# Gated linear attention and a three-way maxout FFN on one core: steps of 128 tokens of two batches in place of 256 tokens of one

## The chip, the core and the metric

The kernel runs on one core of a Trainium2 chip. Its engines are TensorE (PE, with PEld for the loading of weights), VectorE (DVE), ScalarE (ACT), GpSimd (POOL) and SyncE (SP), and each takes its instructions in order. The DMA engines are shared and are fed by queues; here SP and ACT issue transfers. The metric is the device time of one execution in microseconds (us).

## What is computed

```python
def _attn_ref(q, k, v, alpha):            # each (4, 8, 768, 48): batch, head, token, dim
    state = np.zeros((B, H, D, D))
    for t in range(S):
        state = alpha[:, :, t, :, None] * state + np.einsum('bhd,bhe->bhde', k[:, :, t], v[:, :, t])
        y[:, :, t] = np.einsum('bhd,bhde->bhe', q[:, :, t], state)
    return y

# x = y, heads side by side: 3072 tokens of 384
h = np.maximum(np.maximum(x @ w1, x @ w2), x @ w3)     # w1, w2, w3: (384, 768)
return h @ w_out                                       # w_out: (768, 384)
```

A linear attention with a decay `alpha` for each token and key dimension, and behind it a feed-forward layer whose hidden value is the largest of three products. Inputs and outputs are float32.

## The kernel before

**Tiling.** A unit is 128 tokens of one batch. Inside it, two neighbouring tokens (R = 2) lie in the free dimension of one partition, so a unit takes 64 partitions, and a tile of 128 partitions holds two units (U = 2). A step `s` is such a tile: 256 tokens in a row of one batch, `c, b = divmod(s, B)`. There are 12 steps: the first 256 tokens of the four batches, then the second, then the third. The two units of a step follow each other in time, so unit 1 needs the state that unit 0 leaves.

**One step.** Each of alpha, k, q and v comes as one load of 384 KB into a ring of four buffers (`load_step`, L94, letter `l`, indices 0 to 3). alpha gives pair products (`m`, L177), logs (`N`, L181) and an inverse (`r`, L186 and L188); a matmul sums the logs (`c`, L202 and L205); `e`, `f` and `g` (L210, L216, L222) take exponentials into the decays for k and q and the gates of the whole unit (`ge`). k and q are scaled (`u`, `w`, `k`, `q`; L192, L196, L228) into float16 tiles, v likewise (`V`, L149), and k and q are turned, by PE and a copy (`T`, `t`) or by a DMA transpose (`D`, L260). Scores (`A`, L273) are masked (`a`, L280). Attention into `yps` has three sources: the state that the other unit's place holds (`X`, `attend_crossed`), the own one and the masked scores (`Y`, `attend`), all on L299; the result is copied to `xT` (`x`).

**The state.** `S` (`update`, L369) multiplies k and v of each unit into `sps`. `s` (`add_state`, L379) adds what was kept, `M` (`gates`, L356) makes the factor `gm`, `z` (`decay_state`, L384) multiplies by it into `kept`, and `y` (`spread_state`, helper lines L143 and L145) copies that as float16 into `st` for the next unit. All four exist once per unit, with tiles of 128x192 for the state; the second unit of the last chunk is left out, which makes 20 of each.

**The feed-forward layer.** `G` (`gate`, L398) is a group of six matmuls of 256 columns for two of the six blocks of 128 hidden units and one of the three weights: index `i` stands for block pair `i // 3` and weight `i % 3`, so each step has nine groups. `h` (`maxed`) casts the first of three to float16 (L143 on ACT, L145 on DVE) and takes the maximum with the others on DVE (L415). `O` (`project`, L424) multiplies with `w_out`, `o` (`store`) scales by a column and sends 128 rows out on SP (L430 by way of L149, L432). Weights come in twelve blocks (`K`, L105 and L108) and are cast to float16 (`W`).

**What sets the order.** The schedule is manual. `ORDER` is a list of pieces, each a letter, an index, an optional engine (`v` DVE, `p` POOL, `a` ACT) and the step: `z0p@3` is the decay of unit 0 of step 3 on POOL. `emit` issues them one after another, so on every engine and in SP's queue the instructions stand in the order of the list. PSUM has eight banks that all results share. `H` pieces are matmuls on zeros.

Of the kernel before, what the change touches and what calls it, by code (L numbers as in the profile page):

```python
# [23 lines left out]
def kernel(  # L24
# [28 lines left out]
    NS = NT // W  # L53
    NQ = 4
    assert DM == H * D and NT == B * S and 2 * D == 3 * C and DM % P == 0
    assert S % W == 0 and U * J == P and (MID + 1) % R == 0
# [35 lines left out]
    def load(n, s):  # L92
        c, b = divmod(s, B)
        nc.sync.dma_start(  # L94
            rings[n][s % NQ].rearrange("j h r d -> j h (r d)"),
            ins[n][b, :, c * W:(c + 1) * W].rearrange("h (j r) d -> j h (r d)", r=R))

    def load_step(s, i, _):
        load("akqv"[i], s)

    def load_weight(i):
        if i < 9:
            w = (moe_w1, moe_w2, moe_w3)[i % 3]
            src = w.rearrange("(f p) j -> p f j", p=P)[:, :, i // 3 * 2 * P:(i // 3 + 1) * 2 * P]
            nc.sync.dma_start(stage[i].rearrange("p (f c) -> p f c", f=NF), src)  # L105
        else:
            src = moe_w_out.rearrange("(j p) m -> p j m", p=P)[:, 2 * (i - 9):2 * (i - 8)]
            nc.sync.dma_start(stage[i].rearrange("p (j m) -> p j m", j=2), src)  # L108
# [18 lines left out]
    sts = [[cpool.tile([P, 2 * HP + 1, D], FP16, name=f"st{b}_{i}") for i in range(2)] for b in range(B)]  # L127

    def clear_padding():
        for st in (st for pair in sts for st in pair):  # L130
            nc.vector.memset(st[:, ::2], 0.0)
        for la in las:
            nc.vector.memset(la.rearrange("p a b c -> p (a b) c")[:, :, D:], 0.0)
        for qk, vt in zip(qks, vts):
            nc.gpsimd.memset(qk.rearrange("p r i a b c -> p (r i a b) c")[:, :, D:], 0.0)
            nc.vector.memset(vt.rearrange("p a b c -> p (a b) c")[:, :, D:], 0.0)
# [83 lines left out]
    def totals(s, *_):  # L220
        gate_of[s] = work.tile([P, HP, U, 2], FP32, name="ge", tag="ge", bufs=8)
# [62 lines left out]
    def held(s, i, x, at, n):  # L284

        b, rows = s % B, slice(64 * i, 64 * (i + 1))
        st = sts[b][x].rearrange("p a d -> p (a d)")
# [16 lines left out]
    def has_state(s, x):  # L304
        return U * (s // B) + x > 0

    def attend_crossed(s, *_):
        for x in range(U):
            y_of[s, x] = bank([P, NF, P], "yps")
        for f in range(NF):  # L310
            for half in range(2):
                at = P * f + 64 * half
                for i in range(2):
                    if has_state(s, 1 - i):
                        for p, st in held(s, i, 1 - i, at, 64):
                            attend_product(s, 1 - i, at, 64, st, asked(s, i, 1 - i, p))

    def attend(s, _, tag):
        vt = vts[s % NQ]
        lats = [lat_of.pop((s, u)) for u in range(U)]  # L320

        def jobs(x, m):
            todo, fs = [], sorted(range(NF), key=lambda f: (P // C * f + m) % 3 == 1)
            fs = [fs[0], fs[2], fs[1]]
            for f in fs if has_state(s, x) else ():
# [27 lines left out]
    def gates(s, x, eng):  # L353
        nxt = gate_of[s][:, :, 1, 0] if x == 0 else gate_of[s + B][:, :, 0, 0]
        gm = work.tile([P, HP], FP32, name="gm", tag="gm", bufs=6)
        engines[eng or "p"].tensor_mul(gm, gate_of[s][:, :, x, 1], nxt)  # L356
        gm_of[s, x] = gm

    def update(s, _, tag):
        qk, vt = qks[s % NQ], vts[s % NQ]  # L360
        xs = range(U) if s + B < NS else range(1)
        for x in xs:
            sps_of[s, x] = bank([P, HP, D], "sps")
        for p in range(HP):
            for r in range(R):
                for x in xs:
# [5 lines left out]
    def add_state(s, x, eng):  # L372
        c, b = divmod(s, B)
        full = work.tile([P, HP, D], FP32, name="full", tag="full", bufs=4)
        full_of[s, x] = full
        if U * c + x == 0:
            copy(eng or "v", full, sps_of.pop((s, x)))
        else:
            nc.vector.tensor_add(full, sps_of.pop((s, x)), kept_of[b, U * c + x - 1])  # L379

    def decay_state(s, x, eng):
        c, b = divmod(s, B)
        kept = kept_of[b, U * c + x] = work.tile([P, HP, D], FP32, name="kept", tag="kept", bufs=6)
        engines[eng or "p"].tensor_mul(kept, full_of.pop((s, x)),  # L384
                                       gm_of.pop((s, x)).unsqueeze(2).broadcast_to([P, HP, D]))

    def spread_state(s, x, eng):
        c, b = divmod(s, B)
        copy(eng or "a", sts[b][1 - x][:, 1::2], kept_of[b, U * c + x])
# [37 lines left out]
    def store(s, x, eng):  # L427
        c, b = divmod(s, B)
        ob = work.tile([P, DM], FP32, name="ob", tag="ob", bufs=5)
        times(eng or "a", ob, ops_of.pop((s, x)), ys_c)  # L430
        row = b * S + (U * c + x) * P
        nc.sync.dma_start(out[row:row + P, :], ob)  # L432

    def warm(_, n, *x):
# [5 lines left out]
        "l": load_step, "K": lambda _, i, *x: load_weight(i), "W": cast_weight, "H": warm,  # L440
# [8 lines left out]
    def emit(order):  # L449
# [6 lines left out]
        l0@0 r0@0 m0v@0 N0@0 H12@0 c0@0 e0@0 l0@1 m0p@1 r0@1 l1@0 u0v@0 k0v@0 r1@0 l2@0 w0v@0  # L456
        N0@1 H8@0 c0@1 f0@0 k1p@0 r1@1 q1v@0 H4@0 T1@0 l0@2 m0v@2 q0v@0 T0@0 f0@1 l2@1 w0v@1
        l1@1 q1v@1 l3@0 N0@2 c0@2 l0@3 l2@2 l1@2 g0@0 r0@2 r1@2 t0v@0 g0@1 l3@1 e0@1 t1v@0 H5@0
        A1@0 K3@0 k1v@1 T1@1 u0p@1 M0p@0 f0@2 a3@0 l3@2 V0a@0 g0@2 q0p@1 t1a@1 k0v@1 A0@0 a0@0
        a1@0 M0p@1 S0@0 s0a@0 T0@1 t0a@1 H4@0 A0@1 m0p@3 z0p@0 s1v@0 a2@0 y0a@0 X0@0 A1@1 N0@3  # L460
        K0@0 q1v@2 c0@3 e0@2 e0@3 a3@1 w0p@2 q0v@2 V0a@1 l2@3 Y0@0 x0a@0 a0@1 x1v@0 W3a@0 f0@3
        u0p@2 k0p@2 g0@3 H5@0 S0@1 s0v@1 T0@2 a1@1 G3@0 k1p@2 a2@1 K1@0 z0p@1 K2@0 y0a@1 h3a@0
        T1@2 s1v@1 V0v@2 X0@1 Y0@1 S0@2 t0a@2 t1v@2 A0@2 A1@2 W0p@0 x1a@1 q1p@3 s0a@2 a1@2 a3@2
        G0@0 a2@2 M0p@2 z0v@2 x0a@1 G3@1 h0v@0 l1@3 M0p@3 G0@1 a0@2 W1a@0 G1@0 l0@5 r0@3 r1@3
        W2p@0 G1@1 y0a@2 X0@2 Y0@2 G2@1 s1v@2 K4@0 w0p@3 q0p@3 G2@0 k1p@3 h1v@0 K6@0 W6p@0 u0v@3
        k0v@3 x1a@2 x0a@2 G2@2 G0@2 h2v@0 W4a@0 G1@2 h0a@1 h1v@1 m0p@5 h2v@1 h0a@2 h1v@2 G4@0
        h4v@0 K7@0 l3@3 V0a@3 T1@3 t1v@3 G6@1 T0@3 t0v@3 G6@2 G4@1 h2v@2 h6a@1 A0@3 h3a@1 h4v@1
        l0@4 m0p@4 W7a@0 G6@0 a0@3 K5@0 W5p@0 G5@0 N0@4 K8@0 a1@3 W8p@0 l1@4 N0@5 c0@5 r0@4
        h6a@0 h5v@0 c0@4 e0@4 A1@3 a3@3 S0@3 s0a@3 G8@2 a2@3 u0p@4 g0@4 z0v@3 k0p@4 G7@0 r1@4
        M1p@0 k1p@4 h7v@0 g0@5 f0@4 K9@0 l2@4 y0a@3 f0@5 s1v@3 h6a@2 M0p@4 w0v@4 G5@1 h5v@1 G8@0  # L470
        h8v@0 l3@4 V0a@4 l1@5 q0p@4 e0@5 X0@3 Y0@3 x1a@3 x0a@3 q1v@4 G7@1 T0@4 t0a@4 l0@6 r0@6
        M1p@1 T1@4 G0@3 S0@4 z1p@0 h7v@1 u0p@5 M0p@5 t1v@4 r0@5 s0v@4 K11@0 A0@4 z0p@4 A1@4 a1@4
        r1@6 l0@7 l0@8 a2@4 a0@4 a3@4 k1p@5 l2@5 K10@0 G3@2 l3@5 G5@2 G1@3 G4@2 y0p@4 m0p@6
        k0p@5 h3a@2 h4v@2 h5v@2 y1a@0 X0@4 Y0@4 h0a@3 r1@5 m0v@7 w0p@5 G7@2 h7v@2 l2@8 l1@6 l2@6
        q1p@5 D1@5 G8@1 h8v@1 h1v@3 x0a@4 x1a@4 G6@3 h6v@3 q0p@5 W11p@0 h8v@2 V0a@5 D0@5 G2@4
        G8@3 G0@4 G1@4 G3@3 N0@6 c0@6 N0@7 h0v@4 h1v@4 W10a@0 W9p@0 s1v@4 z1p@1 f0@6 w0v@6 S0@5
        s0v@5 q0v@6 e0@6 c0@7 f0@7 g0@7 M1p@3 u0v@6 k0p@6 l2@7 l3@6 O0@1 h3a@3 o0a@1 D0@6 l1@7
        q1p@6 k1p@6 O1@2 D1@6 z0v@5 s1v@5 g0@6 M1p@2 o1a@2 e0@7 O0@0 o0a@0 A1@5 a3@5 A0@5 a1@5
        G3@4 G2@3 y1a@1 l1@8 O1@1 r0@8 l0@9 a0@5 l3@8 a2@5 h2v@3 G7@3 G5@4 h7v@3 o1a@1 h8v@3
        y0p@5 O0@2 X0@5 q1p@7 V0a@6 S0@6 Y0@5 m0p@8 z1p@2 r1@8 w0v@8 h2v@4 s0v@6 M0v@6 G4@4  # L480
        h3v@4 h4v@4 G4@3 h4v@3 z0p@6 r0@7 N0@8 r1@7 w0p@7 o0a@2 x1a@5 u0v@7 l0@10 x0a@5 G6@5
        h6a@5 l0@11 r0@9 G7@5 h5v@4 A1@6 a2@6 a3@6 A0@6 a0@6 a1@6 G5@3 s1v@6 y1v@2 G0@5 k0p@7
        G1@5 h0a@5 h1v@5 y0p@6 G3@5 h3a@5 h5v@3 G2@5 M0v@7 X0@6 Y0@6 x1v@6 x0a@6 c0@8 e0@8 G5@5
        f0@8 l3@7 r0@11 q0v@8 u0p@8 k0v@8 G4@5 g0@8 k1p@7 G3@6 l1@9 h4v@5 h3a@6 G4@6 V0a@7 z1v@3
        O1@0 q0p@7 D0@7 M1p@4 z1p@4 G7@6 D1@7 h2v@5 G5@6 l3@10 o1a@0 h5v@5 h4v@6 q1p@8 k1p@8
        S0@7 s0v@7 y1a@4 z0v@7 G0@6 h0a@6 O0@3 D0@8 h7v@5 s1v@7 A0@7 a0@7 D1@8 A1@7 G6@6 V0a@8
        G8@5 m0p@10 l2@9 a2@7 o0a@3 y1p@3 a1@7 h8v@5 h6a@6 G8@6 m0p@9 N0@9 c0@9 f0@9 G6@4 N0@10
        g0@9 M0p@9 M1p@5 y0p@7 O1@3 a3@7 G2@6 h7v@6 X0@7 M0p@8 m0p@11 o1a@3 h6a@4 e0@9 k1p@9
        h5v@6 h8v@6 Y0@7 x1v@7 A1@8 a2@8 x0a@7 r1@9 S0@8 w0p@9 a3@8 r0@10 l2@10 A0@8 G1@6 h1v@6
        a1@8 G0@7 G2@7 G6@7 h2v@6 h6a@7 G7@7 a0@8 G3@7 s0v@8 q0v@9 z0v@8 q1p@9 u0p@9 r1@10 l3@11  # L490
        G5@7 w0p@10 h7v@7 G7@4 G8@7 l1@10 h3a@7 y0a@8 G8@4 l1@11 G4@7 h7v@4 h8v@4 h0a@7 G1@7
        h1v@7 N0@11 l3@9 c0@10 e0@10 X0@8 Y0@8 f0@10 u0p@10 k0p@9 D1@9 q0v@10 x1a@8 l2@11 k0p@10
        x0v@8 V0a@9 O0@5 D0@9 O1@5 o0a@5 c0@11 r1@11 g0@10 z1p@5 G0@8 e0@11 k1p@11 q1p@10 D0@10
# [49 lines left out]
```

## Time and profile before

Three runs took 155.5, 153.03 and 154.42 us, median 154.42.

| of the profiled execution | |
|---|---|
| its own time | 153.8 us |
| span in the profile | 152.0 us |
| mean granted TensorE clock | 0.998 |
| busy: PE / PEld / DVE / ACT / POOL | 140.6 / 107.6 / 117.1 / 86.6 / 76.1 us |
| moved by DMA | 32.52 MB, mean 214 GB/s |
| queue of SP (q1) | 72,576 packets, 84.6% of 16 engines' span |
| 648 matmuls of the expert groups, L398 | 76.2 us busy |
| 144 matmuls of the projection, L424 | 25.7 us busy |

Shares are of the span. The span is measured inside the profiled execution, from the first instruction to the last; the execution's own time is 1.8 us longer. A busy engine is not one at its peak, since matmuls overlap. In lists of groups the columns are line, engine, operation, output and inputs with their shapes and count, then busy time, the mean of one in ns, and the idle time just before with what ended it.

### The profile page before, as it was taken

The numbers are of one execution on the slowest core, as the hardware profiler recorded it, in microseconds if no ns is written. First come the engines' busy times: TensorE is split into PE (matmuls) and PEld (weight loads), VectorE is DVE, ScalarE is ACT, GpSimd is POOL, SyncE is SP. The second block draws the span as 40 slices with busy tenths as digits, with TensorE's granted clock in tenths as the row PEclk, the third lists the DMA queues.
The fourth block names the chain that finished last, engine by engine and source line by source line (L and its number), as shares of the span: only waits on it lengthen the run. The fifth ranks groups of instructions, "written<-read, shape, count | busy, mean of one in ns | idle before, by whom it ended". The sixth has DMA issues, their size and how long they took to land.

```text
span 152.0 us, 6282 instructions
## 1 busy us (share of the span) xinstructions
PE 140.6 (93%) x2722; PEld 107.6 (71%) x2722; DVE 117.1 (77%) x212; ACT 86.6 (57%) x177; POOL 76.1 (50%) x109
## 2 busy tenths in 40 slices
PE   6977969899998999899899999999999999999990
PEld 2434647689786887478688778887878887878650
DVE  5299895899998897699967988969986960977820
ACT  3667968555879377847347666269853406031371
POOL 5327782792698976683736728665865020000000
PEclk9999999999999999999999999999999999999999
DMA  4999999998999999999999999999968301112235
GB/s 121 317 323 306 242 298 334 248 347 236 348 261 308 312 302 207 192 302 257 316 269 240 220 163 293 285 236 196 149 163 44 87 4 56 52 32 76 92 140 182
DMA packets 72891, 32.52 MB, mean 214 GB/s; under 512 B 65440, under 2 KB 72864, under 8 KB 72864
## 3 DMA queue, kind: packets, MB, share of 16 engines
q1 hardware_dynamic: 72576, 31.99, 84.6%
q8 instruction: 21, 0.34, 0.9%
q10 hardware_dynamic: 288, 0.13, 0.5%
q14 instruction: 6, 0.05, 0.1%
HBM read 23.73 MB, written 4.72 MB: 187 GB/s over the span
## 4 chain that ended last, share of the span: by engine, by line
PE 69%; SPq 9%; DMA 7%; POOL 6%; DVE 2%; issue 2%; ACT 2%; DVEq 0%; ACTq 0%; POOLq 0%
PE gps L398 41%; PE ops L424 14%; SPq L94 9%; PE yps L299 6%; DMA ws<-in_moe_w_dram 4%; PE aps L273 3%; POOL qk L228 3%; DMA qkT<-qk 3%; PE sps L369 2%; PE tps L252 2%; DVE h L415 1%; POOL wo L145 1%; PE lps L202 1%; POOL ka L192 1%; POOL qa L196 1%
## 5 line engine op out<-in xcount | busy, mean ns | idle before, releaser
L398 PE MATMUL gps<-xT,wcat 128*128 128x256 f16 x648 | 76.2, 273 | 1.7 <-ACT wcat L143 0.8
L398 PEld LDWEIGHTS <-wcat 128*128 128x128 f16 x648 | 61.5, 98 | 11.2 <-ACT wcat L143 1.3
L280 DVE TENSOR_TENSOR lat<-aps,cp 128x512 f16<-128x512 f32 x48 | 30.6, 683 | 3.8 <-PE aps L273 3.5
L415 DVE TENSOR_TENSOR hT<-gps,h 128x512 f16<-128x512 f32 x36 | 24.0, 686 | 9.7 <-PE gps L398 5.4
L415 DVE TENSOR_TENSOR h<-gps,h 128x512 f16<-128x512 f32 x36 | 24.4, 687 | 4.1 <-PE gps L398 1.8
L143 ACT CAST h<-gps 128x512 f16<-128x512 f32 x28 | 16.3, 587 | 18.2 <-PE gps L398 12.2
L424 PE MATMUL ops<-wo,hT 128*128 128x384 f16 x144 | 25.7, 326 | 0.3 <-ACT h L143 0.3
L149 ACT ACTIVATE ob<-ops,c 128x384 f32<-128x384 f32 x24 | 13.8, 582 | 17.0 <-PE ops L424 17.0
L424 PEld LDWEIGHTS <-hT 128*128 128x128 f16 x144 | 13.8, 98 | 8.4 <-issue 0.5
L143 ACT CAST xT<-yps 128x384 f16<-128x384 f32 x20 | 8.9, 480 | 9.8 <-PE yps L299 9.6
L384 POOL TENSOR_TENSOR kept<-full,gm 128x192 f32<-128x192 f32 x14 | 8.0, 570 | 10.9 <-PE aps L273 4.9
L149 ACT ACTIVATE vt<-rv,c 128x768 f16<-128x768 f32 x11 | 10.3, 936 | 4.3 <-DMA rv<-in_v_dram 4.3
L177 POOL TENSOR_TENSOR pa<-ra 128x384 f32<-128x384 f32 x9 | 9.1, 1014 | 6.2 <-DMA ra<-in_alpha_dram 6.2
L437 PE MATMUL wps<-wo 128*128 128x512 f16 x38 | 10.9, 433 | 1.2 <-DVE wo L510 1.2
L228 POOL TENSOR_TENSOR qk<-rk,ic 128x384 f16<-128x384 f32 x10 | 10.6, 1060 | 2.2 <-ACT ic L210 1.9
L192 POOL TENSOR_TENSOR ka<-rk,ra 128x384 f32<-128x384 f32 x8 | 8.0, 1001 | 6.6 <-DMA rk<-in_k_dram 5.2
L273 PE MATMUL aps<-qkT 48*64 48x128 f16 x384 | 8.9, 220 | 1.8 <-DVE qkT L145 0.5
L299 PE MATMUL yps<-lat,vt 64*32 64x128 f16 x768 | 9.7, 221 | 0.3 <-issue 0.3
L273 PEld LDWEIGHTS <-qkT 48*64 48x64 f16 x384 | 6.2, 106 | 4.7 <-issue 1.7
L186 ACT ACTIVATE ra<-ra 128x384 f32<-128x384 f32 x12 | 6.1, 519 | 5.9 <-DMA ra<-in_alpha_dram 4.8
L228 POOL TENSOR_TENSOR qk<-ka,ic 128x384 f16<-128x384 f32 x7 | 7.2, 1027 | 3.9 <-issue 1.3
L356 POOL TENSOR_TENSOR gm<-ge 128x4 f32<-128x4 f32 x16 | 4.3, 275 | 9.3 <-ACT ge L222 9.3
(54 smaller groups left out, 172.7 us busy)
## 6 DMA issues: line engine op xcount, KB each, us to landing
ra<-in_alpha_dram SPq DMA_DIRECT2D x12, 384.0 KB, 5.1
rk<-in_k_dram SPq DMA_DIRECT2D x12, 384.0 KB, 5.6
rq<-in_q_dram SPq DMA_DIRECT2D x12, 384.0 KB, 5.4
rv<-in_v_dram SPq DMA_DIRECT2D x12, 384.0 KB, 5.6
out_dram<-ob SPq DMA_DIRECT2D x24, 192.0 KB, 2.8
ws<-in_moe_w_dram SPq DMA_DIRECT2D x9, 384.0 KB, 6.3
ws<-in_moe_w_out_dram SPq DMA_DIRECT2D x3, 384.0 KB, 5.7
qkT<-qk SPq DMA_TRANSPOSE x14, 4.8
```

Source lines behind the costliest of these rows:

```text
L94: nc.sync.dma_start(rings[n][s % NQ].rearrange("j h r d -> j h (r d)"), ins[n][b, :, c * W:(c + 1) * W].rearrange("h (j r) d -> j h (r d)" ...
L143: nc.scalar.copy(out=dst, in_=src)
L149: nc.scalar.mul(dst, src, col)
L192: engines[eng or "p"].tensor_mul(near_of[s, "k"], raw("k", s, 0), raw("a", s, 1))
L228: engines[eng or "p"].tensor_mul(dst.rearrange("p a b c -> p (a b) c")[:, :, :D], near_of.pop((s, n)) if r == 0 else raw(n, s, 1), dec_of[ ...
L273: nc.tensor.matmul(aps[i][cols, a * R + r, :], qkT[rows, r, 1, p, cols], qkT[rows, :, 0, p, cols], start=True, stop=True)
L280: nc.vector.tensor_mul(lat_of[s, u][:, i].rearrange("p (a r) t -> p a r t", r=R), aps_of[s, u][i].rearrange("p (a r) t -> p a r t", r=R), ...
L299: nc.tensor.matmul(y_of[s, x][rows, f, :], lhs, rhs, start=new, stop=last)
L398: nc.tensor.matmul(gps[:, j, :], wcat[:, f, g, jj * P:(jj + 1) * P], xT[:, f].rearrange("p u t -> p (u t)"), start=(f == 0), stop=(f == NF ...
L415: nc.vector.tensor_max(h, gps, h_of[s, i - 1])
L424: nc.tensor.matmul(ops, hT_of[s][:, jj, u * P:(u + 1) * P], wo16[:, jj, :], start=(jj == 0), stop=(jj == NJ - 1))
L437: nc.tensor.matmul(wps, blank[:, :P], blank, start=True, stop=True)
```

## The change

A step is now 128 tokens of two batches: `c, g = divmod(s, NG)` with `NG = 2`, unit `u` is batch `2g + u`, and there are again 12 steps, two for each of six chunks of tokens. The units of a step no longer depend on each other; the state that a step leaves is asked for by step `s + 2`. The two units of a load lie in different batches, so each load is two transfers of 64 partitions (indices 0 to 3 the lower half, 4 to 7 the upper). A load or a weight block with the engine letter `a` is issued on ACT's queue instead of SP's: 40 of 96 halves and two of twelve blocks. `M`, `z` and `y` exist once per step and work on both units (tiles of 128x384), ten of each; `s` remains one for each unit, since each has its own bank. Steps 0 and 1 have no state and no `X` piece. The last two steps have no `S`. `ORDER` is new as a whole, with other engines for some pieces: of the 36 first casts of `h`, 16 are on DVE in place of 8, of the 24 copies `x` 12 in place of 4, of the 24 scalings `o` 5 in place of none, and POOL makes 20 of the 24 `q` products in place of 13. The number of matmuls of each kind is the same, but for `H`, 35 in place of 38.

```diff
+    NG = B // U
...
-    def load(n, s):
-        c, b = divmod(s, B)
-        nc.sync.dma_start(
-            rings[n][s % NQ].rearrange("j h r d -> j h (r d)"),
-            ins[n][b, :, c * W:(c + 1) * W].rearrange("h (j r) d -> j h (r d)", r=R))
-
-    def load_step(s, i, _):
-        load("akqv"[i], s)
+    def load_step(s, i, eng):
+        n, u, (c, g) = "akqv"[i % 4], i // 4, divmod(s, NG)
+        (nc.scalar if eng == "a" else nc.sync).dma_start(
+            rings[n][s % NQ][u * J:(u + 1) * J].rearrange("j h r d -> j h (r d)"),
+            ins[n][U * g + u, :, c * P:(c + 1) * P].rearrange("h (j r) d -> j h (r d)", r=R))
...
-    sts = [[cpool.tile([P, 2 * HP + 1, D], FP16, name=f"st{b}_{i}") for i in range(2)] for b in range(B)]
+    sts = [[cpool.tile([P, U, 2 * HP + 1, D], FP16, name=f"st{g}_{i}") for i in range(2)] for g in range(NG)]
...
-        b, rows = s % B, slice(64 * i, 64 * (i + 1))
-        st = sts[b][x].rearrange("p a d -> p (a d)")
+        c, g = divmod(s, NG)
+        rows = slice(64 * i, 64 * (i + 1))
+        st = sts[g][c % 2][:, x].rearrange("p a d -> p (a d)")
...
-    def has_state(s, x):
-        return U * (s // B) + x > 0
+    def has_state(s):
+        return s >= NG
...
-    def gates(s, x, eng):
-        nxt = gate_of[s][:, :, 1, 0] if x == 0 else gate_of[s + B][:, :, 0, 0]
-        gm = work.tile([P, HP], FP32, name="gm", tag="gm", bufs=6)
-        engines[eng or "p"].tensor_mul(gm, gate_of[s][:, :, x, 1], nxt)
-        gm_of[s, x] = gm
+    def gates(s, _, eng):
+        gm = work.tile([P, U, HP], FP32, name="gm", tag="gm", bufs=3)
+        engines[eng or "p"].tensor_mul(gm, gate_of[s].rearrange("p a u b -> p u a b")[:, :, :, 1],
+                                       gate_of[s + NG].rearrange("p a u b -> p u a b")[:, :, :, 0])
+        gm_of[s] = gm
...
+    def decay_state(s, _, eng):
+        kept = kept_of[s] = work.tile([P, U, HP, D], FP32, name="kept", tag="kept", bufs=3)
+        engines[eng or "p"].tensor_mul(kept, full_of.pop(s),
+                                       gm_of.pop(s).unsqueeze(3).broadcast_to([P, U, HP, D]))
+
+    def spread_state(s, _, eng):
+        c, g = divmod(s, NG)
+        copy(eng or "a", sts[g][1 - c % 2][:, :, 1::2], kept_of[s])
...
-        l0@0 r0@0 m0v@0 N0@0 H12@0 c0@0 e0@0 l0@1 m0p@1 r0@1 l1@0 u0v@0 k0v@0 r1@0 l2@0 w0v@0
-        N0@1 H8@0 c0@1 f0@0 k1p@0 r1@1 q1v@0 H4@0 T1@0 l0@2 m0v@2 q0v@0 T0@0 f0@1 l2@1 w0v@1
...
+        l4@1 H10@0 l4@0 H2@0 H1@0 l1a@0 l6a@0 l0@0 m0v@0 r0@0 N0@0 c0@0 e0@0 H1@0 l5@0 k1v@0
+        u0p@0 g0@0 f0@0 l5a@1 H12@0 k0v@0 l0@1 r0@1 l2@0 q1v@0 m0v@1 r1@0 w0v@0 q0v@0 r1@1 N0@1
+        c0@1 g0@1 f0@1 l2@1 T1@0 t1v@0 l0@3 l4@2 l0@2 m0p@2 l6@1 l1@2 N0@2 e0@1 q1p@1 T0@0 t0v@0
+        A0@0 l3a@1 w0v@1 l4@3 m0v@3 q0p@1 l1@1 u0p@1 A1@0 a3@0 a1@0 a0@0 l0a@4 c0@2 e0@2 k1v@1
+        l3@0 l7@0 k0v@1 K1@0 W1p@0 l5@2 k1p@2 u0p@2 V0a@0 H4@0 H4@0 a2@0 T1@1 r0@2 T0@1 l2@2
+        Y0@0 t0v@1 t1a@1 A0@1 K3@0 W3p@0 x0v@0 x1a@0 G1@0 a1@1 k0v@2 S0@0 s1v@0 a0@1 g0@2 r1@2
...
```

The rest of the diff carries `s`, `x` and the batch of a unit through `store`, `update`, `add_state` and `attend` in the same way.

## The prediction

> **What bounds the kernel now.** I read the page's busy shares and slices first, then the chain of waits, the timeline of SP's queue, the windows of the first 20 us, and last the groups and the waits of POOL.
>
> The busy shares, and the slices (3.8 us each):
>
> ```profile
> PE 140.6 (93%) x2722; PEld 107.6 (71%) x2722; DVE 117.1 (77%) x212; ACT 86.6 (57%) x177; POOL 76.1 (50%) x109
> ...
> PE   6977969899998999899899999999999999999990
> ...
> DVE  5299895899998897699967988969986960977820
> ...
> DMA  4999999998999999999999999999968301112235
> ```
>
> PE is near full from the eighth slice to the end, DVE is full beside it for most of the middle, and the DMA engines are full for the first 29 slices, to 110 us. So three resources run close together, and what is left to win is in the first 30 us. The chain says what holds the start:
>
> ```profile
> 14.01 1.15 SPq L94
> ...
> 15.20 6.43 DMA ws<-in_moe_w_dram
> 21.66 0.84 ACT wcat L143
> ...
> 22.55 0.83 PE gps L398 x6
> ...
> 28.57 0.76 issue
> 29.32 1.38 PE gps L398 x11
> ...
> 140.58 7.82 PE ops L424 x48
> ```
>
> SP issues loads back to back until 15.20, the first weight block lands at 21.64, is cast, and the first expert matmul starts at 22.55; from 29.32 PE hardly stops. The columns of the next view, SP's timeline, are start, duration, queue and line:
>
> ```profile
> 1.87 1.44 SPq L94 DMA_DIRECT2D rk<-in_k_dram  x1
> ...
> 15.20 1.89 SPq L105 DMA_DIRECT2D ws<-in_moe_w_dram  x1
> 17.14 0.49 SPq L94 DMA_DIRECT2D rv<-in_v_dram  x1
> ```
>
> An issue can take 0.49 us; the long ones are SP being held while the engines drain. Windows (last three columns: granted clock, DMA share, GB/s) show the drained rate:
>
> ```profile
> 5.00:10.00 5.00, 4.15 (x27) 1.75 (x26) 2.96 (x6) 3.48 (x9) 2.30 (x2) 1.00 1.16 322
> 10.00:15.00 5.00, 3.87 (x71) 2.47 (x74) 4.66 (x9) 3.58 (x10) 2.74 (x4) 1.00 1.15 314
> 15.00:20.00 5.00, 4.73 (x164) 3.09 (x163) 4.53 (x9) 4.06 (x9) 4.11 (x6) 1.00 0.94 255
> ```
>
> With loads alone the engines move 322 GB/s, so a 384 KB load (393,216 bytes) takes **1.22 us**. From 15 us, with weights in the queue, the share drops to 0.94. Over the first thirteen transfers, from 4.53 (the first alpha, where ACT's L186 starts) to 21.66, the pace is 17.13 / 12 = **1.43 us**.
>
> **Loads in halves, two queues, new order.** 48 loads become 96 halves with the same bytes; 40 of them and two weight blocks go to ACT's queue. Counting along the orders, in whole transfers: before, the blocks stand at K3 13, K0 15, K1 17, K2 18; after, at K1 11.5, K3 13.5, K0 16.5, K5 17.5, K4 20, K2 21. So the first block comes earlier and the last of the early ones later, but the new order has more expert groups (six matmuls, 0.67 us in the run x36 in 4.04) to do before K2: G1, G3, G0 of step 0, G0 and G5 of step 1, and so on, nine in all. I compare one point that both reach: ten groups, attention of steps 0 to 2 and the update of step 2. Before: six groups and attention are done at 31.79 by the chain, four more groups make 34.5. After: K2 is the sixth block and has 30 halves ahead of it. No row shows a half load. Bound below by half a load, 0.61 us, above by a whole one, 1.22 us; the nearest row is the load itself, whose time goes with its bytes, so I take 0.61. At 0.61 for the 28 halves after the first pair and 1.43 for six blocks, K2 lands at 4.53 + 17.1 + 8.6 = 30.2; cast 0.83, G2 of step 1 0.67, attention of step 2 1.10 (as at 30.70 in the chain), update 0.4: 33.2, a gain of 1.3. With all at 1.22 it is 31.9 (gain 2.6), with all at 1.43 it is 36.1 (loss 1.6). I take a gain of **1.0**, below 1.3 because nine of the 30 halves stand behind ACT's own work. Step 0 itself isn't late: its values are complete after 10.5 transfers, 4.53 + 9.5 x 1.3 = 16.9, plus 0.94 for vt and some 3 us for attention and xT is 21, where K1 is cast.
>
> **What ACT pays.** An issue on its queue is shown twice:
>
> ```profile
> 0.77 0.39 ACTq L114 DMA_DIRECT2D cp<-cp  x1
> ```
>
> and 0.46 for the next; 42 x 0.42 = 17.6 us. The new order takes from ACT 8 casts of h (8 x 0.587), 8 of xT (8 x 0.48), 5 scalings of ob (5 x 0.58), one weight cast (0.84) and some copies of the state (9 x 0.352 to 4 of some 0.51): 13.3 us. ACT goes from 86.6 to 73.3 busy plus 17.6 issuing, 60% of the span, hidden in its idle time. A load also waits for its ring slot, and behind it stand ACT's next pieces: behind the upper k half of step 6, the two inverses of step 3, for which POOL's q waits. If an issue on ACT held it as the whole loads hold SP (medians 0.74 to 1.45, mean 1.05), 26 us more would put ACT at DVE's present share; PE now waits 2.1 us for DVE. So 0 to +2.1, and I take **+0.3**, nearer to the ACTq rows.
>
> **What DVE gets.** 8 casts of h (0.687), 8 of xT (0.552), 5 of ob (about 0.56), 2 pair products (0.556), less 7 products into q (0.65), 5 state decays (0.568) and small ones: +5.5 us, to 122.6. Its cover is 35 us of idle time, but in 35 to 75 us DVE is busy 35.3 of 40. Half of the increase could fall uncovered there: 0 to +2.8, and I take **+0.3**, as the rows summed along both orders give DVE like work per PE work from 30 us on.
>
> **One decay and one copy per step.** Twenty gates, decays and copies become ten:
>
> ```profile
> L384 POOL TENSOR_TENSOR kept<-full,gm 128x192 f32<-128x192 f32 x14 | 8.0, 570 | 10.9 <-PE aps L273 4.9 <-DVE full L379 3.4 <-DVE gm L356 2.4
> ...
> L356 POOL TENSOR_TENSOR gm<-ge 128x4 f32<-128x4 f32 x16 | 4.3, 275 | 9.3 <-ACT ge L222 9.3
> ```
>
> A decay of 128x384 costs about 1.0 on POOL (the 128x384 products of L177 take 1.014), so 14 x 0.57 = 8.0 becomes 9 x 1.0; gates go from 4.3 to some 1.7, and a double copy lies between 0.345 (128x192) and 0.83 (128x768). POOL also takes 7 more q products, 7.1 us. So no engine time is won, only order: 20 us of POOL's waits in these rows hold what is queued behind, and the state now has two steps until it is asked for, where before the first unit's had to reach the second inside its step. PE paid for POOL twice after 29.32:
>
> ```profile
> 46.90 1.19 PE L252 MATMUL tps<-cp,qk 128*128 128x128 f16 x16 [0.74 <-POOL qk L228]
> ...
> 63.67 0.65 PE L273 MATMUL aps<-qkT 48*64 48x128 f16 x32 [0.44 <-DMA qkT<-qk]
> ```
>
> (the second by a transpose issued behind POOL's work). So 0 to -1.2; I take **-0.4**. The work on the state is hidden by the expert groups between an update and the attention that asks for it, 9 to 29 in the order; between the decay and that attention there are 2 (step 3) to 18. Two groups are 1.3 us, and decay and copy take some 1.5, so there the cover is thin, and a late POOL would cost PE that 1.5 once.
>
> **Nothing for the rest.** Matmuls of all kinds keep their number, but for 38 warming ones that become 35 ahead of the bound part. Eight output projections still end the order, with one scaling (0.58) and one store (2.8) behind.
>
> **Sum:** -1.0 + 0.3 + 0.3 - 0.4 = -0.8. The profiled execution took 153.8 us, 152.0 of it span; that gives 153.0. The median shown is 154.42, 0.6 higher; from it I get 153.6. I forecast **153.3**, with 150.5 to 155.5 as this case's own range.
>
> **Rivals.** *A half load costs more than half a load* (slower). Place: the load stream. Before, the last load is issued at 100.16 and lands some 5.4 later, 105.6; the new order asks for its last one with some 35 us of PE work left, a point that the old one passes near 111.5. So 6 us are spare over 96 halves: it decides from 0.61 + 0.06 = 0.67 us a half. A quarter of the way from 0.61 to 1.22, at 0.76, the stream is 14.5 us longer, 8.5 of them uncovered: 162.3; halfway, +29 gives 177. For it: the DMA slices have no room before 110 us. Against: the same bytes and the same rows of 384 B. [...] Its chance is the largest of the rivals on that side.
>
> *The full gain* (faster). The second queue keeps the engines full, all transfers at 1.22, and both POOL stops go: -2.6 - 1.2 = -3.8, so 150.0. For it: the drop to 0.94 comes when SP alone stands in one issue of 1.89. Against: DVE is no freer.
>
> *ACT is held by its queue.* SP's longest single issue, of a weight block, took 4.2 us; ACT now issues two blocks. If both hold it so, PE runs on for about 2 us of free banks and stops 2.2 twice: 157.7. Against: ACT's queue is short.
>
> **Chances.** Forecast 0.36, full gain 0.28, dear halves 0.28, ACT held 0.08. A measurement of this kernel tells about 2% from no change: 151.3 and 157.5. Faster: 0.25 of the full gain and 0.07 of the forecast's low end, 0.32. Slower: 0.26 of the dear halves, 0.05 of ACT, 0.02 of the forecast, 0.33. Same: 0.35. The range 148.0 to 162.5 leaves out the upper half of the dear halves and a little below, under 0.2.
>
> **What would show it.** Right: the first expert matmul near 21, ten groups and attention of step 2 by 33.5, 310 GB/s or more in 5 to 15 us, PE idle under 3 us after that. Dear halves: 200 to 260 GB/s there and values of step 0 after 19 us. ACT held: ACTq issues over 1 us with casts of h behind them. Wrong altogether: PE stopping in the middle for DVE, or the state's copy on the chain.

## The result and the profile after

The change makes the kernel slower: 180.19 us median (177.43 to 183.64) beside 153.72 for the kernel before on the same chip, a ratio of 1.162 with a 95% interval from 1.142 to 1.181. Ratios here and below compare the faster executions of the two kernels alone, so they are not the ratios of the medians. The profiled execution took 177.4 us, 175.6 of it span. First the page of the kernel after: its busy shares, and rows of its 40 slices (now 4.4 us each).

```profile
PE 146.2 (83%) x2719; PEld 109.4 (62%) x2719; DVE 121.8 (69%) x217; ACT 76.5 (44%) x150; POOL 80.0 (46%) x97
...
PE   7387674997954889699878968899979999999991
...
DMA  5999999997999999999999978998999811003053
GB/s 128 220 208 228 230 181 279 257 247 148 241 214 238 210 219 202 246 219 242 223 271 276 147 157 235 190 170 213 176 237 205 149 49 49 0 4 133 22 207 134
```

The DMA row is as full as before, but PE has holes up to the middle, and the GB/s row goes with it: the engines are busy and move little (mean 185 GB/s over the span, before 214). The windows of the first 20 us (busy time of PE, PEld, DVE, ACT, POOL; then granted clock, DMA share, GB/s) answer to those shown of before:

```profile
5.00:10.00 5.00, 1.21 (x10) 0.53 (x9) 0.56 (x1) 1.05 (x2) 0.06 (x1) 0.78 1.26 222
10.00:15.00 5.00, 5.00 (x16) 1.76 (x14) 3.22 (x6) 2.79 (x7) 0.94 (x1) 0.54 1.29 214
15.00:20.00 5.00, 4.07 (x70) 2.70 (x69) 3.04 (x5) 2.05 (x5) 3.53 (x4) 1.00 1.30 226
```

The DMA share is higher than before (1.26 against 1.16) and the rate a third lower (222 against 322 GB/s). A half load of 196,608 bytes takes 0.89 us at the mean of 221 GB/s. The PE row of 10 to 15 us misleads: 16 matmuls fill 5 us, at a granted clock of 0.54. The chain of waits of the kernel after, in order of time (start, duration, what):

```profile
16.44 6.05 DMA rv<-in_v_dram
...
25.87 7.26 DMA ws<-in_moe_w_dram
33.15 9.15 DMA rv<-in_v_dram
42.33 0.94 ACT vt L148
43.31 0.79 PE yps L299 x64
```

From 16 to 42 us three transfers follow each other, with a few issues of SP between the first and the second, and behind the third stands attention of step 2: it ends at 44.1, where before it ended near 31.8. Before, the chain left the loads at 21.64, and had one transpose more that landed at 63.6; here it comes back to them up to the transpose that lands at 129.5, and only from 130 us on is it PE's own. PE's last matmul ends at 172.0, where before it ended at 148.4. Of these 23.6 us, 18.0 are added stops of PE (9.9 of them before 55 us), and 5.6 are work: PE is busy that much longer with the same matmuls, less three warming ones. The two groups that make most of the 5.6 are the expert matmuls (79.8 against 76.2 us) and the warming ones (517 ns each against 433); both fall partly in stretches where the granted clock is down (0.50 in 30 to 35 us).

Of the waits of SP (us in total, times, longest) the largest of a load on a landing:

```profile
SPq L95 <- DMA rk<-in_k_dram: 10.5, 7, 4.7
```

SP now stands at a load until an earlier load has landed, and issuing one half takes it 0.60 us or more (the timeline), where the shortest whole loads before took 0.39 to 0.49. In the trace the landings of the 148 transfers are told on eight semaphores, 18 or 19 on each. The transfer before on the same semaphore, on whichever queue it was, is the seventh to tenth before for 115 of 140, and no issue ends before that one has landed (123 of the 123 whose landing is told). The chain shows it: the v load that ACT issued at 16.44 landed at 22.49, and SP's next load starts at 22.50. Eight whole loads were 3.1 MB; eight halves are 1.6 MB, over two queues.

### The profile page after: what moved, and what is told of

Read it like the earlier page. It is cut to its first block, busy times and chain, and to the rows that moved or that the text cites. A ratio compares the mean times of both kernels' runs of the same rounds, so it can differ in the third digit from the quotient of the medians.

```text
span 175.6 us, 6311 instructions
## 1 busy us (share of the span) xinstructions
PE 146.2 (83%) x2719; PEld 109.4 (62%) x2719; DVE 121.8 (69%) x217; ACT 76.5 (44%) x150; POOL 80.0 (46%) x97
## 4 chain that ended last, share of the span: by engine, by line
DMA 47%; PE 35%; ACT 4%; DVE 4%; SPq 2%; issue 2%; ACTq 2%; POOL 1%; DVEq 0%; POOLq 0%
PE gps L399 21%; DMA rv<-in_v_dram 13%; DMA rq<-in_q_dram 11%; PE ops L425 9%; DMA ws<-in_moe_w_dram 9%; DMA ra<-in_alpha_dram 8%; DMA qkT<-qk 4%; DMA out_dram<-ob 3%; PE yps L299 3%; PE aps L272 2%; SPq L95 1%; ACT vt L148 1%; ACTq L95 1%; DVE h L144 1%; SPq L104 1%
## 5 line engine op out<-in xcount | busy, mean ns | idle before, releaser
L399 PE MATMUL gps<-xT,wcat 128*128 128x256 f16 x648 | 79.8, 278 | 7.0 <-POOL wcat L144 2.7
L142 ACT CAST h<-gps 128x512 f16<-128x512 f32 x20 | 11.7, 585 | 20.8 <-PE gps L399 12.9
L148 ACT ACTIVATE ob<-ops,c 128x384 f32<-128x384 f32 x19 | 10.8, 580 | 19.1 <-PE ops L425 14.5
L227 POOL TENSOR_TENSOR qk<-qa,ac 128x384 f16<-128x384 f32 x10 | 10.1, 1012 | 5.8 <-ACT ac L215 3.0
L144 DVE CAST h<-gps 128x512 f16<-128x512 f32 x16 | 11.0, 686 | 1.7 <-PE gps L399 1.1
L385 POOL TENSOR_TENSOR kept<-full,gm 128x384 f32<-128x384 f32 x9 | 8.1, 895 | 8.8 <-DVE gm L359 8.7
L227 POOL TENSOR_TENSOR qk<-rk,ic 128x384 f16<-128x384 f32 x8 | 8.0, 1000 | 7.8 <-DMA rv<-in_v_dram 3.6
L227 POOL TENSOR_TENSOR qk<-rq,ac 128x384 f16<-128x384 f32 x10 | 10.4, 1037 | 2.4 <-ACT ac L215 1.5
L176 POOL TENSOR_TENSOR pa<-ra 128x384 f32<-128x384 f32 x7 | 7.0, 999 | 9.5 <-DMA ra<-in_alpha_dram 9.5
L227 POOL TENSOR_TENSOR qk<-ka,ic 128x384 f16<-128x384 f32 x9 | 9.1, 1015 | 3.5 <-ACT ge L221 2.2
```

Of the source, the lines that this page charges most:

```text
L142: nc.scalar.copy(out=dst, in_=src)
L144: engines[eng].tensor_copy(out=dst, in_=src)
L148: nc.scalar.mul(dst, src, col)
L227: engines[eng or "p"].tensor_mul(dst.rearrange("p a b c -> p (a b) c")[:, :, :D], near_of.pop((s, n)) if r == 0 else raw(n, s, 1), dec_of[ ...
L399: nc.tensor.matmul(gps[:, j, :], wcat[:, f, g, jj * P:(jj + 1) * P], xT[:, f].rearrange("p u t -> p (u t)"), start=(f == 0), stop=(f == NF ...
```

## The experiments

Two theories stood against each other at first. *The partitions*: a transfer that fills only the lower or only the upper 64 partitions moves fewer bytes per us. *The queues and the order*: twice as many transfers, on two queues of which one is ACT's, and weights that come late. All times are medians, and ratios are to the kernel before on the same chip. The diffs are shortened to what they change.

| run | what it is | us | ratio (95%) |
|---|---|---|---|
| after | the change | 180.2 | 1.162 (1.142 to 1.181) |
| b_halves | before, loads in 64-partition halves, SP | 171.4 | 1.111 (1.103 to 1.120) |
| b_heads | before, loads in halves by heads, SP | 155.2 | 1.012 (1.003 to 1.021) |
| b_two | as b_heads, every second half on ACT | 179.9 | 1.169 (1.151 to 1.187) |
| a_sp | after, all on SP | 180.5 | 1.176 (1.160 to 1.193) |
| a_heads | after, halves by heads, two queues | 162.1 | 1.042 (1.031 to 1.053) |
| a_heads_sp | as a_heads, all on SP | 158.6 | 1.017 (0.994 to 1.041) |
| a_spread | after, halves on every second partition | 165.5 | 1.076 (1.069 to 1.083) |
| a_whole | after's order, whole loads, SP | 157.5 | 1.025 (1.004 to 1.046) |
| a_whole_sep | as a_whole, state in two instructions | 157.7 | 1.026 (1.016 to 1.036) |
| a_whole_cast | as a_whole, two casts later on POOL | 156.4 | 1.026 (1.019 to 1.032) |
| a_whole_k7 | as a_whole_cast, K7 earlier | 157.3 | 1.034 (1.022 to 1.045) |

In a_heads, a_spread, a_whole and what is made from them, every tile gets the same number of bytes in rows of 384 B, but other tokens than the change puts there; all instructions on the engines stay.

### Loads alone

```diff
+ for i in range(12): whole(i)                           # SP
+ for i in range(12): lower(i), upper(i)                 # SP
+ for i in range(12): lower(i)                           # SP; then all upper(i)
+ for i in range(12): lower(i) on SP, upper(i) on ACT
+ for i in range(12): heads 0-3, heads 4-7               # 128 partitions, SP; then SP and ACT
+ for i in range(12): partitions 0::2, partitions 1::2   # SP
```

> This kernel only moves inputs (it computes nothing; its output is a constant): seven phases of 4.7 MB each, with a pause between, all in rows of 384 B. 1: whole loads on SP. 2: halves of 64 neighbouring partitions on SP, lower and upper in turn. 3: the same halves on SP, twelve lower ones, then twelve upper ones. 4: lower ones on SP, upper ones on ACT at the same time. 5: halves of 128 partitions by four heads each on SP. 6: the same, one on SP and one on ACT. 7: halves of 64 partitions that take every second partition, on SP. Theory A (64 neighbouring partitions are the price): 1, 5, 6 and 7 near 320 GB/s, 2 and 3 near 215, 4 in between or near 320. Theory B (two queues disturb each other): 4 and 6 low, all others near 320. Theory C (more and smaller transfers are the price): 2 to 7 alike, near 220, only 1 at 320.

Windows inside each phase (no PE here: DVE, POOL, clock, DMA share, GB/s), in the order of the diff:

```profile
5.00:15.00 10.00, 0.00 (x0) 0.00 (x0) 1.00 1.17 324
30.00:40.00 10.00, 0.00 (x0) 0.00 (x0) 1.00 1.28 236
50.00:62.50 12.50, 0.00 (x0) 0.00 (x0) 1.00 1.33 199
85.00:92.50 7.50, 0.00 (x0) 0.00 (x0) 1.00 1.28 236
102.50:112.50 10.00, 0.00 (x0) 0.00 (x0) 1.00 1.11 297
122.50:130.00 7.50, 0.00 (x0) 0.00 (x0) 1.00 1.17 323
142.50:150.00 7.50, 0.00 (x0) 0.00 (x0) 1.00 1.07 282
```

Whole loads run at 324 GB/s. All lower and then all upper halves run at 199, which is 0.99 us a half; taking lower and upper in turn gives 236 (0.83 us), on one queue as on two. Halves of the same size and row length keep 297 on 128 partitions from one queue and 323 from two, as fast as whole loads, and 282 on 64 partitions spread over all. That is the pattern of theory A; by B or C the heads would have been slow as well. The DMA share tells them apart as well: it is 1.28 and 1.33 at 236 and 199 GB/s, and 1.07 to 1.17 at 282 to 324, so in the slow phases the engines are busy longer for the same bytes. The kernel after, with its 221 GB/s, lies between 199 and 236; its halves come only partly in turn.

The second set tells the number of partitions from their place, and has quarters of loads for the wait on the eighth transfer.

```diff
+ partitions 0-63, all loads; 32-95; 64-127; 0-31        # SP
+ quarters by two heads on 128 partitions                # SP; then SP and ACT
```

> Loads alone, twelve of 384 KB a phase, all else left out. Phases in order on SP: whole loads; halves on partitions 0-63; on 32-95; on 64-127; loads of 32 partitions (0-31); quarters by two heads on all 128 partitions; the same quarters alternately on SP and ACT. The theory that it matters which partitions a load covers (lower and upper half are served by different halves of the paths): 0-63 and 64-127 at 190 to 205 GB/s, 32-95 at 260 to 325 although it has 64 neighbouring partitions as well, 0-31 at 200 or below. The rival that the number of partitions sets it (64 descriptors rows instead of 128): all three kinds of 64 alike near 200, 0-31 near 100 to 130. On the wait for the eighth transfer before: if 8 transfers in flight are too few once each is a quarter (8 x 96 KB), quarters on SP fall to 230 or below and the two queues don't help; if not, they keep 285 or more.

The windows of 0-63, 32-95 and 64-127:

```profile
25.00:40.00 15.00, 0.00 (x0) 0.00 (x0) 1.00 1.32 200
50.00:65.00 15.00, 0.00 (x0) 0.00 (x0) 1.00 1.05 280
77.50:90.00 12.50, 0.00 (x0) 0.00 (x0) 1.00 1.32 206
```

Partitions 32-95 are 64 neighbours too, and run at 280. So it is neither the number 64 nor that they are neighbours; it is being all in the lower half (200) or all in the upper half (206). That the halves are served by different paths, as the theory has it, no run shows; the runs show the rates. (Nor need 280 be the limit of 64 partitions: with every second partition, at 282, one issue follows the other on SP's timeline, two of them 1.31 us in every 1.36, and their 393,216 bytes in 1.36 us are 289 GB/s.)

The quarters answered neither of my two cases: on SP they ran at 190 GB/s because each took 0.50 us to issue, four in 2.00 on SP's timeline (98,304 bytes in 0.50 us is 197 GB/s); on two queues they reached 242. The loads on 0-31 were of the same 96 KB and came at 180 to 213, so they may be bound by issue as well and tell nothing.

### Halves in the old order

```diff
-  nc.sync.dma_start(ring[n], whole(n, s))
+  for u in range(2): nc.sync.dma_start(ring[n][64 * u:64 * (u + 1)], half(n, s, u))          # b_halves
+  for u in range(2): nc.sync.dma_start(ring[n][:, 4 * u:4 * (u + 1)], heads(n, s, u))        # b_heads
```

> The kernel before, each load cut into a lower and an upper half of 64 partitions, both on SP, in the old order. Theory A: the DMA rate in 5 to 15 us falls from 318 to about 215 GB/s and the time rises to 170 to 185 us. Theory B (two queues): as before, 152 to 156. Theory C (more transfers): 170 to 185 as well. Theory D (the new order and the joint state work cost the time): 152 to 157.

> The kernel before, each load cut into two halves of four heads on all 128 partitions, both on SP, in the old order: as many transfers of the same size and the same rows as in the run with lower and upper halves. Theory A: rate and time as before, 152 to 156 us, at most some more for issuing. Theory C: about 215 GB/s, 170 to 185. Theories B and D: 152 to 156.

With everything else as before, halves on 64 partitions cost 11.1%, the same halves by heads 1.2%. The window of 5 to 15 us of b_halves has the marks of the loads in turn:

```profile
5.00:15.00 10.00, 7.34 (x49) 3.52 (x48) 5.47 (x10) 6.21 (x16) 2.35 (x2) 0.92 1.27 240
```

So the old order has most of the loss too, once its loads are cut at partition 64. Halving a load without that costs 1.2%, inside the 152 to 156 us expected.

### Cheap halves in the new order, and the queues

```diff
-  rings[n][s % NQ][u * J:(u + 1) * J] <- batch 2g + u
+  rings[n][s % NQ][:, 4 * u:4 * (u + 1)] <- heads 4u to 4u + 3       # a_heads
+  rings[n][s % NQ][u::2] <- batch 2g + u                              # a_spread
-  (nc.scalar if eng == "a" else nc.sync).dma_start(
+  nc.sync.dma_start(                                                  # a_sp, a_heads_sp
```

> The changed kernel in its order and queues, but each half load takes four heads of one batch on all 128 partitions (the attention then works on wrongly placed tokens; all shapes, counts and waits are the same). Theory A: the rate in 5 to 15 us returns to some 320 GB/s and the time to 150 to 157 us, which is what the rest of the change is worth. Theory B, C or D: stays at 172 or more.

> The changed kernel with one thing different: each half load still has 64 partitions, the same bytes, queue and place in the order, but is put to every second partition instead of to the lower or upper 64 (tokens land in other rows than the reference's). If neighbouring partitions of one half are what costs, the start fills at 258 to 290 GB/s and the time is near that of the halves by heads, 158 to 166. If any 64-partition load costs it, 220 GB/s at the start and 177 to 183.

> The changed kernel with the halves by heads (128 partitions, wrongly placed tokens, as in the run before), and all its loads and weight blocks on SP's queue instead of 40 and two on ACT's. Theory E (two queues in one rotation: each transfer waits for the landing of the eighth transfer before it in program order, whichever queue that is on, so ACT stands for landings of SP and SP for issues that are late on ACT): 153 to 157 us, no more stops of ACT at loads. Theory F (the new order and the joint state work are slower by themselves): 159 to 163, as with two queues.

> The changed kernel as it is, halves of 64 neighbouring partitions and the right data, with all loads and weight blocks on SP. Theory A alone (the halves are the price): 175 to 182 us. Theory E beside it: 168 to 175. Theory F: no change, near 179.

Halves by heads take 18 of the 26 us back with the order and both queues as in the change; halves on every second partition, which still have 64 partitions, take back 15. So where the halves lie is the cause of the larger part, shown in both orders and by two cures. But 162.1 misses the 150 to 157 that were expected with cheap halves, so something else in the change costs as well.

The second queue is worth nothing while the halves are dear (a_sp 1.176, after 1.162). With cheap halves all on SP is the better one in the medians, 158.6 against 162.1, but the intervals touch, so a cost of ACT's queue here is seen in single stops and not shown in the whole. One such stop in a_heads (profiled execution, 163.1 us): ACT stands at a load behind an earlier load's landing, with the cast that PE waits for queued behind it. From its timelines of ACT and PE:

```profile
77.06 0.41 ACTq L96 DMA_DIRECT2D rv<-in_v_dram  x1
77.56 0.59 ACT L143 CAST h<-gps 128x512 f16<-128x512 f32 x1 [2.82 <-DVE lat L280]
...
78.20 5.40 PE L400 MATMUL gps<-xT,wcat 128*128 128x256 f16 x48 [1.89 <-ACT h L143]
```

The load that ACT issues at 77.06 had to wait for a q load that SP had issued at 71.92 and that landed at 77.04 by the chain, the seventh transfer before it; the bracket names DVE, which had long been done.

In the old order, which was written for one queue, the second queue does far more harm:

```diff
-            nc.sync.dma_start(
+            (nc.scalar if u else nc.sync).dma_start(    # b_two, on b_heads
```

> The kernel before with halves by heads, the first on SP and the second on ACT at the same place of the old order. Theory E: ACT stands at loads for landings, 157 us or more. If only the issuing on ACT counts (48 x 0.4 us in ACT's idle time): 154 to 157. Theory F: as with both on SP, 155.

```profile
7.89 0.45 ACTq L96 DMA_DIRECT2D ra<-in_alpha_dram  x1
...
19.44 0.52 ACT L183 ACTIVATE la<-pa 128x384 f16<-128x384 f32 x1 [5.03 <-DMA rq<-in_q_dram]
```

On ACT's timeline the second half of step 1's alpha is issued only at 7.89, behind ACT's own work for step 0, where SP had issued the first half by 1.75; and before 19.44 ACT has computed nothing for 5.03 us, in which it issued three loads (1.4 us). A load on a computing engine's queue comes no earlier here than that engine's work in front of it. SP is held too: its v load at 11.64 starts when the late alpha half has landed, the same moment at which ACT's next inverse starts. The ratio is 1.169 with halves that alone cost 1.2%, far from the 157 us that theory E named as the least.

### The order with whole loads

```diff
-  nc.sync.dma_start(rings[n][s % NQ][u * J:(u + 1) * J], batch 2g + u)
+  if (n, s) not in loaded: nc.sync.dma_start(rings[n][s % NQ], 256 tokens of one batch)   # a_whole
-  kept = full * gm                       # 128x384, and gates and copy likewise
+  for u in range(U): kept[:, u] = full[:, u] * gm[:, u]                                   # a_whole_sep
```

> The changed order and the joint state work with whole loads of 128 partitions on SP, each at the place of the earlier of its two halves (256 tokens of one batch, so wrongly placed tokens for the attention; all counts of the other work are the same). What is left of the change is order, engines and state. Theory F: 158 us or more. If these parts are worth what the prediction gave them: 150 to 155. Theory E: near the run with halves by heads on SP, some 1% below it.

> The new order with whole loads on SP (as in the run with 157.5 us), with the gate, the decay and the copy of the state issued as two instructions per step again, one per unit. My prediction gave the joint instructions 0 to 1.2 us, 0.4 as the value: 157.5 to 158.7 if it holds, with POOL some 3 us busier. The rival that the joint state costs, since the first unit now waits for both: 156.5 or below.

With whole loads the new order costs 2.5%, just under theory F's 158 us. The joint state is worth nothing that can be measured (the intervals are 1 to 2% wide on each side, so the 0.4 us of the forecast can't be told from nothing): 157.7 with separate instructions against 157.5, though POOL is 3.2 us busier (82.8 against 79.6). Windows of before and of a_whole, first 55 us and the next 95 (before's two lines first):

```profile
0.00:55.00 55.00, 48.50 (x1048) 34.98 (x1049) 45.47 (x87) 37.10 (x77) 35.18 (x50) 1.00 1.01 287
55.00:150.00 95.00, 92.14 (x1676) 72.58 (x1673) 71.65 (x127) 49.52 (x101) 40.89 (x60) 1.00 0.79 174
```

```profile
0.00:55.00 55.00, 43.68 (x891) 31.61 (x892) 41.22 (x79) 29.68 (x60) 32.84 (x44) 0.97 1.04 296
55.00:150.00 95.00, 94.81 (x1823) 75.38 (x1822) 79.71 (x139) 44.63 (x89) 46.71 (x55) 1.00 0.71 163
```

The new order loses 4.8 us of PE's work in the start and wins 1.1 back later. In the second window PE rests 0.2 us, where before it rested 2.9; but 1.6 of these lie behind the last matmul of before, at 148.4, so its stops there were 1.3. So the later part of the new order is a little better and its start is bad, which is the reverse of what I had forecast.

Two runs looked for the place in the start. In a_whole POOL stands 2.69 us for weight block K1, with two products of step 2 queued behind its cast, and PE then waits for step 2's last product:

```profile
20.42 0.82 POOL L149 CAST wcat<-ws 128x768 f16<-128x768 f32 x1 [2.69 <-DMA ws<-in_moe_w_dram]
...
26.75 1.89 PE L256 MATMUL tps<-cp,qk 128*128 128x128 f16 x16 [1.94 <-DVE qk L232]
```

```diff
-  K1@0 W1p@0 l5@2 k1p@2 u0p@2 V0a@0 ... K3@0 W3p@0 ... w0p@2 A1@1
+  K1@0 l5@2 k1p@2 u0p@2 W1p@0 V0a@0 ... K3@0 ... w0p@2 W3p@0 A1@1     # a_whole_cast
-  K6@0 h0v@2 ... G6@0 h6a@0 K7@0 W7a@0
+  K7@0 K6@0 h0v@2 ... G6@0 h6a@0 W7a@0                                # a_whole_k7, on a_whole_cast
```

> The new order with whole loads on SP (157.5 us, span 155.3 in its profiled run), with two weight casts moved back on POOL: that of K1 behind the products k1p and u0p of step 2, that of K3 behind w0p of step 2. There POOL stood 2.67 us until K1 had landed at 20.40, with the two products behind it, and PE then waited 1.94 us at 26.75 for the last product of step 2. If the order of POOL's queue is what loses the start with whole loads, the turn of step 2 comes 2 to 3 us earlier than 26.75 and the run takes 154.5 to 156. The rival is that the next blocks are late anyway (POOL waited 1.02 and 0.30 us for landings at 27.30 and 28.43): the turn comes earlier, PE stops at the expert groups behind it instead, and the time stays at 157 to 158.

```profile
25.35 1.09 PE L256 MATMUL tps<-cp,qk 128*128 128x128 f16 x16 [0.67 <-DVE qk L232]
...
49.58 0.83 PE L404 MATMUL gps<-xT,wcat 128*128 128x256 f16 x6 [1.85 <-ACT wcat L147]
```

The stop at 26.75 shrank, attention of step 2 ended 2.6 us earlier (35.4 against 37.9), and the ratio did not move: PE stood longer behind that, 1.85 us for block K7 (1.58 in a_whole), and its work in the first 55 us is 44.0 us against 43.7. In the new order K7 is the 35th of 60 transfers, before it was the 23rd.

> The kernel with whole loads and the two casts moved back (156.4 us, ratio 1.026), with one thing more: the load of weight block K7 is issued just ahead of that of K6, as transfer 30 of 60 where it was 35 (the kernel before has it as 23). In that run PE stopped 1.85 us at 49.58 for the cast of K7, the largest stop after 30 us. If the place of the weight blocks in the load stream is what the new order loses the rest by, that stop goes, nothing as large takes its place, and the time is 154 to 155, ratio 1.01 to 1.017. If the loads that are pushed back (step 6's alpha and v, step 5's q, step 4's k) are as late for their own users, PE stops 1 to 2 us for step 4 instead, and the time stays at 156 to 157.

```profile
46.74 0.90 PE L277 MATMUL aps<-qkT 48*64 48x128 f16 x32 [1.81 <-ACT qkT L147]
```

The stop for K7 is gone and one of nearly the same size stands 3 us ahead of it, at the scores of step 3; the ratio is 1.034. (This execution was 1.8 us behind already at attention of step 0, ahead of every piece that was moved, so single executions differ at the start by as much as the stops do.) So neither of these two moves is a cure by itself; each only changed who waits. The stream of loads is not behind in bytes: the windows above have 296 GB/s for the new order and 287 for the old one. What the bytes are for differs: the new order asks for the alphas of steps 3 and 4 ahead of the v of step 0, and for K2 as transfer 22 where it was 18. No run took these back, so the 2.5% are placed (the first 55 us) and not resolved.

No kernel here beats the one before. One transfer that fills all 128 partitions from two batches may take away the price of the halves, an estimate from whole loads (324 GB/s) and halves by heads (297 to 323); it was not tried.

## Why the prediction was wrong, point by point

**The step that failed** is the price of a half load. I bounded it by 0.61 and 1.22 us and took 0.61, because the nearest row was the whole load, "whose time goes with its bytes". That row only has loads that cover both halves of the partitions, so it could not show the cost that decides, which is that of filling one half of the partitions. Measured: 0.83 us with halves in turn, 0.99 without, 0.89 in the kernel's own start.

**The rival had it.** *A half load costs more than half a load* gave 0.67 us as the point from which it decides; beyond that, 96 halves at 0.89 lie 96 x 0.22 = 21 us over, which gives 175. Both of its marks came: 222 and 214 GB/s where it said 200 to 260, and values of step 0 at 21.64 (vt begins) where it said after 19. So its place, the load stream, and its cause were right. That my line "halfway, +29 gives 177" is so near the 177.4 of the profiled execution is in part luck: it is for 0.92 us, and with cheap halves some 8 of the 26 us stay. Its way of paying was right only in part. It charged only the end of the stream, and the last load is indeed issued at 135.1 instead of 100.2; but on the chain the last load lands at 101.0, and 9.9 of PE's 18.0 us of added stops come before 55 us, so the loads were paid for all along. Its chance was too low, and as its time I took a quarter of the way instead of half: I let "the same bytes and the same rows of 384 B" weigh against it, which the heads and spread runs show to be no argument, as they have both and are fast.

**Theory A**, as I worded it before the runs of loads, had 64 neighbouring partitions as the price. That was too wide: 0 to 63 and 64 to 127 ran at 200 and 206 GB/s, but 32 to 95 at 280. The kernel, at 0.89 us a half, came out between halves in two blocks (0.99) and halves in turn (0.83). The turn itself gains 236 / 199, so 19%, on one queue or two.

**The start, -1.0.** With dear halves it is a loss: ten groups and attention of step 2 are done at 44.1, where the forecast had 33.2, an update of 0.4 included. Even where the transfers are cheap the gain was wrong in sign: a_heads is that far at 35.4 and a_whole at 37.9, and before had 34.5. In a_heads the cast of K2, the sixth block, starts at 30.92, so there the forecast landing at 30.2 was nearly right. What failed is the part behind it: I put one expert group between K2 and the attention, but PE works through five from 30.60 to 34.0. The sum left out what stands in queues behind late landings, as POOL's two products behind K1's cast in a_whole. The first expert matmul, forecast near 21, was at 25.1 in the kernel after and at 20.7 to 21.3 in a_spread, a_heads and a_whole: that part held wherever the halves were cheap.

**ACT, +0.3.** An issue was priced at 0.42 us from rows of constants; halves took 0.60 to 0.65, some 8 us more of ACT's time over 40 of them; with all on SP (a_sp) the time is no better. What I missed is the coupling: the wait for an earlier transfer, which held ACT for a landing on SP's queue (at 77.06 in a_heads). The rival *ACT is held by its queue* had the issue times as its reason, and the longest was 0.96; the stops came by the landings.

**DVE, +0.3**, and the size of its work: 121.8 busy against 122.6 forecast. With whole loads (DVE 121.1) PE rests 0.2 us in the 95 us after 55, so there its work found its cover and cost nothing.

**Joint state and POOL's stops, -0.4.** The first half can't be told from nothing by the a_whole_sep run. The second, PE's stops: with whole loads they fell from 1.3 to 0.2 us behind 55 us, inside the 1.2 I allowed, but rose from 0.8 to 2.2 between 30 and 55 us. Which of the new order's moves does either was not tested.

## What to carry to other kernels

A transfer's price had two parts here that its byte count does not show: which partitions it fills (on SP alone, 192 KB took 0.99 us all in one half, at 199 GB/s, and 0.66 by heads on all 128, at 297), and how long its issue holds the queue (0.50 us for 96 KB on all 128, which ran at 190 GB/s on one queue). Before a tile is split by partitions, look whether each piece still reaches both halves of the 128; in this kernel a split by heads, which leaves each piece on all 128, costs 1.2% where the split at partition 64 costs 11.1%. A DMA share that rises (1.16 to 1.26) while GB/s falls (322 to 222) was the mark of it here. And a stop that goes when one piece is moved, with the time unchanged, says that the stop was a symptom: look for the stretch, not the line.

## What was not expected of the hardware

Lower and upper halves in turn do better than the same halves in two blocks (236 against 199 GB/s), and the second queue adds nothing to it (236). A half on 64 partitions takes its queue 0.60 to 0.65 us to issue, a quarter on 128 partitions 0.50, so a stream of 96 KB transfers on one queue ends at 190 GB/s with the engines not full (share 0.85). Late loads went with slower matmuls too: PE was busy 1.2 of the 5 us from 5 to 10, and from 10 to 15 the granted clock was 0.54; before, it was busy 4.2 of the same 5 us, and the clock stayed at 1.00.
